# Third patterns of the integer exponential made in place by an adding DMA, with a newly searched order of work, in a fused attention and gated-FFN kernel

## The chip, the cores and the metric

The kernel runs on one core of a Trainium2 chip. The metric is the device time of one execution in microseconds (us). The engines are PE (matmul), ACT (activations, here nearly all exponentials), DVE (vector), POOL (GpSimd) and SP (which here only issues DMAs); each works through its own list of instructions in order, and semaphores order the engines among each other.

## The reference

`x` is 2048 x 512 in bf16. The result mixes an attention block and a gated feed-forward block by a gate for each row:

```python
g = sigmoid((x * gate_w).sum(-1, keepdims=True))
# attention: 32 heads of 16
qkv = x @ wqkv                       # 2048 x 1536
scores = einsum("bhqd,bhkd->bhqk", q, k) * 16 ** -0.5
o = einsum("bhqk,bhkd->bhqd", softmax(scores), v)
a = o @ wo
# feed-forward, F = 1376, without a nonlinearity
b = ((x @ w_gate) * (x @ w_up)) @ w_down
return g * a + (1 - g) * b
```

The exponentials of the scores are the bulk: 32 heads x 2048 x 2048.

## The kernel before

**Tiles.** PE is used as eight tiles of 64 rows by 32 columns. An operation of the helper `pe64` (L1616, its matmuls are recorded at L1620) is four matmuls, one for each column group, in row half 0 or 1; the two halves run beside each other. All products have 512 columns and land in one of eight PSUM banks. Bank 7 holds the attention output of the group in work, the others serve scores and the remaining products.

**Groups and steps.** The attention is 32 groups: four chunks of 512 queries, four blocks of eight heads, and two halves of such a block (four heads). A group has 16 steps, one for each tile of 128 keys, 512 steps in all. A step makes four score tiles of 128x512 (one for each head, `scores`, L1625) and from them four tiles of exponentials, which PE then multiplies with the values (`pv`, L1646).

**Two ways to an exponential.**

- Kind A: ACT reads one or two PSUM banks and writes exp as bf16 (`exp`, L1718). The four tiles are multiplied with the values once (`ps<-PT,Vp`, `ps<-xT,Vp` and so on: the results lie wherever room is, in `PT` and in the bytes of weights and inputs that are no longer needed). That is 8 matmuls a step.
- Kind D: DVE adds a constant to the scaled score and stores it as int16 (`dpass`, L1754); these 16 bits read as bf16 are a rough exponential, "pattern 0". Patterns 1, 2 and 3 are pattern 0 plus 32, 64 and 96 in int16, each in a buffer of its own, made by DVE (`copy`, L1760, one instruction of 128x2048 or half of it) or by POOL (L1764, two int16 taken as one int32). PE multiplies pattern 0 with the values (`Vp`) and patterns 1 to 3 with values scaled by 2^(-v/4) (`Vs`), so that the four rough curves average out. That is 32 matmuls a step, 24 of them on `Vs`. Only the key tiles in `dks` (six of 16) may take this way. The buffers are the eight of `DB` and later the bytes of `wv` and `wk`.

**The rest.** The projections, the feed-forward products and the output products are cut into short slices and put between the steps ("fill"). Their PSUM banks are emptied by DVE. For each pair of groups the denominators go through DRAM: two small DMAs, a reciprocal, a write to `rscr`, a broadcast back into `rb` (`rbc`, L1912) and a multiplication on POOL (L1923).

**What sets the order.** The order of each engine's instructions is worked out when the program is built, by a model of the chip in the class `_Sched`. It goes forward in time and at each moment gives each free engine one piece of work. `s_a` and `s_d` place scores for the two kinds of steps, `try_act` an exponential, `dve_pass` a pass, `copy_dve` and `try_pool` the copies, `v_job` a product with the values. Its choices depend on fixed durations and latencies and on the numbers of `PAR`. Most of these are tables of pairs (count, value): the time is cut into entries of 4 us, and each value holds for so many entries. Some that matter here: `dl` (how many steps of a group may be of kind D), `dend` (how near to the end of a group no new D step begins), `alook`, `dlook` (how many scores may be ahead of their readers), `acc` (below). The products of a group with the values wait until the group's turn in bank 7. The program then has exactly this order on each engine, with a semaphore wait for each dependence; on the chip an engine never passes over an instruction that is not ready.

**The adding DMA.** The code for it is in the kernel before, but with `acc` at 0 it is never used. Where the number of D steps of a group is at or below `acc`, the step's pattern 3 gets no buffer of its own. Its copy leaves the list (`next_d`, L218), and when pattern 0 has been read by both copies and by both its products (five references, `y_unref`, L506), POOL issues a DMA that adds a constant row of 96 to the buffer in place (`acc_pool`, L960, `accum`, L1768):

```python
def acc_pool(self):
    e, deps, _ = self.accq.pop(0)
    op = self.hw.accum(e.buf, deps + [self.last4]) if self.hw else None
    self.pool_v = self.lock_v = self.now + self.par["aiss"]                  # 0.9
    t = self.dma_v = max(self.pool_v + self.par["alat"], self.dma_v + 2.65)  # 3.9
    for r in (0, 1):
        self.vq[r].append((t, e, 3, [op]))      # the products with pattern 3, from t on

def accum(self, buf, deps):
    src = bass.AP(c.tensor, c.offset, [[0, 128], [1, 2048]])
    return self.P.dma("pool", lambda e: e.dma_start(self.db[buf], src, accum_op=ALU.add), ...)
```

`last4` is DVE's last copy before it in the planned order; POOL waits for it. With `acc` set, the prologue also writes the constant row to DRAM (a memset on POOL, two small DMAs on SP), and `rbc` waits for that.

Of the kernel before, what the change touches and what calls it, by code (L numbers as in the profile page):

```python
# [136 lines left out]
class _Sched:  # L137
# [167 lines left out]
    def s_a(self, r):  # L305
# [20 lines left out]
        t = self.now + 0.385 + 0.056  # L326
# [6 lines left out]
    def s_d(self, r):  # L333
# [22 lines left out]
        t = self.now + 0.385 + 0.056  # L356
# [363 lines left out]
    def try_act(self):  # L720
# [51 lines left out]
        dur = 0.833e-3 * 512 * n + 0.051  # L772
# [10 lines left out]
        t = self.now + dur + 0.12 + 0.05  # L783
# [75 lines left out]
    def dve_pass(self, now):  # L859
# [9 lines left out]
        if self.dready and self.dready[0][0] <= now and (mate or not hold):  # L869
# [12 lines left out]
            dur = 0.065 + 0.533 * n  # L882
# [4 lines left out]
            t = self.now + dur + 0.083  # L887
# [661 lines left out]
class _Hw:  # L1549
# [376 lines left out]
    def prologue(self):  # L1926
# [119 lines left out]
        if self.par["acc"]:  # L2046
# [10 lines left out]
 'acc': 0,  # L2057
# [3 lines left out]
 'alook': ((13, 2), (5, 6), (8, 4), (6, 2), (9, 4), (3, 5), (21, 2), (3, 3), (3, 2), (1, 4), (5, 2), (18, 5),  # L2061
# [4 lines left out]
 'amax': ((7, 5), (35, 4), (6, 5), (81, 4), (6, 5), (45, 4)),  # L2066
 'amin': ((7, 3), (6, 2), (13, 4), (6, 2), (9, 3), (3, 2), (6, 4), (2, 2), (22, 3), (28, 4), (5, 3), (18, 4),
          (7, 3), (5, 4), (5, 2), (19, 4), (5, 3), (5, 4), (9, 3)),
 'apick': ((38, 0), (6, 1), (3, 0), (6, 1), (2, 0), (2, 1), (4, 0), (12, 1), (1, 0), (12, 1), (5, 0), (1, 1),
           (5, 0), (14, 1), (11, 0), (25, 1), (14, 0), (6, 1), (13, 0)),  # L2070
 'ares': ((5, 1), (6, 2), (3, 1), (21, 2), (3, 1), (6, 2), (7, 1), (1, 2), (8, 1), (17, 2), (15, 1), (6, 0),
          (24, 2), (9, 1), (9, 0), (22, 2), (18, 1)),
 'await': ((2, 0.05), (10, 0), (6, 0.05), (5, 0), (6, 0.2), (3, 0), (3, 0.2), (3, 0.1), (3, 0.2), (3, 0),
           (7, 0.05), (1, 0.2), (8, 0.05), (11, 0), (3, 0.2), (6, 0), (3, 0.4), (6, 0.05), (3, 0.1), (10, 0),
           (5, 0.4), (4, 0.2), (10, 0.05), (1, 0.4), (3, 0), (15, 0.05), (2, 0.2), (19, 0.05), (3, 0.4),
# [56 lines left out]
 'hold': 1,  # L2132
 'klead': 0.9,
 'kp': [1, 4, 7],
 'lg': [3, 4],
 'mmarg': 0.6,
 'ndum': 7,
 'npre': 0,
# [85 lines left out]
```

## Time and profile before

| | us |
|---|---|
| median of 3 runs | 710.07 |
| lowest, highest | 707.67, 713.38 |
| the profiled execution | 708.04 |
| its span, first to last instruction | 706.3 |
| ACT busy in it | 684.8 |
| DVE busy | 645.9 |
| POOL busy | 450.7 |

The TensorE clock was granted in full (1.00) throughout. A line such as `L1718 ACT ACTIVATE PT<-ps 128x1024 bf16<-128x1024 f32 x328 | 326.8, 1087 | ...` is a group of 328 instructions of line 1718 that read PSUM and write the tile PT; they kept ACT busy for 326.8 us together, and one of them lasted 1087 ns. Instructions of ACT overlap at their ends, so the first number is less than 328 times the second. Since helpers record the operations, the line alone tells little; the names of the tiles tell which step it is.

### The profile page before, as it was taken

To read this page: it belongs to the slowest core of one execution; us is meant where nothing else is said; L and a number is where in the kernel's file an instruction comes from. 1 tells how busy PE (TensorE), PEld (TensorE's weight loads), DVE (VectorE), ACT (ScalarE), POOL (GpSimd) and SP (SyncE) were. 2 spreads that over 40 slices of the span, in tenths; PEclk is the share of its full clock that TensorE was granted. 3 is DMA by queue.
4 is the path that set the end of the run, shared out by engine and by line. 5 is a ranking of instruction groups with operands and counts; after the bars stand their busy time and mean duration, and the time that the engine had idled before them with its cause. 6 is when DMAs were issued, how large, how long until landed. Compare 5 with 4: busy or idle time off the path is not lost.

```text
span 706.3 us, 47734 instructions
## 1 busy us (share of the span) xinstructions
PE 692.3 (98%) x22103; PEld 358.7 (51%) x22103; DVE 645.9 (91%) x1060; ACT 684.8 (97%) x820; POOL 450.7 (64%) x351
## 2 busy tenths in 40 slices
PE   8999999999999999999999999999999999999997
PEld 4564555554444545554554445555553555555553
DVE  5999999899999999999998998999999978989985
ACT  6899999999999999999999999999999999999994
POOL 3365658877464666655675747777666788487630
PEclk9999999999999999999999999999999999999999
DMA  9202341003010100001000010100001010000101
GB/s 156 69 6 57 78 107 36 6 20 94 16 35 5 35 18 23 28 11 28 13 23 23 15 33 19 36 13 13 27 7 40 12 36 24 14 23 18 29 19 33
DMA packets 33752, 22.97 MB, mean 33 GB/s; under 512 B 19500, under 2 KB 30156, under 8 KB 33552
## 3 DMA queue, kind: packets, MB, share of 16 engines
q1 hardware_dynamic: 32416, 18.86, 11.1%
q8 instruction: 173, 2.83, 1.6%
q0 software_dynamic: 176, 0.53, 0.3%
q10 hardware_dynamic: 960, 0.52, 0.3%
q14 instruction: 27, 0.22, 0.1%
HBM read 11.71 MB, written 2.36 MB: 20 GB/s over the span
## 4 chain that ended last, share of the span: by engine, by line
PE 90%; DVE 3%; ACT 3%; issue 1%; DMA 1%; ACTq 0%; DVEq 0%
PE ps L1620 90%; DVE DB L1754 2%; ACT xT L1718 1%; ACT PT L1718 1%; DVE DB L1760 1%; DMA DB<-in_A_x_dram 1%; ACT wu L1718 0%; DVE wv L1754 0%; DVE oc L1830 0%; DVE hT L1902 0%; PE ps L2017 0%; ACTq L1933 0%; DVE wu L1813 0%; ACT wd L1718 0%; ACT QM L2030 0%
## 5 line engine op out<-in xcount | busy, mean ns | idle before, releaser
L1620 PE MATMUL ps<-QM,KT 64*32 64x512 bf16 x8192 | 496.6, 379 | 4.2 <-issue 1.3
L1764 POOL TENSOR_TENSOR DB<-DB,cadd 128x512 int32<-128x512 int32 (+1 forms) x207 | 280.2, 1373 | 146.9 <-DVE DB L1760 62.0
L1718 ACT ACTIVATE PT<-ps 128x1024 bf16<-128x1024 f32 (+1 forms) x394 | 358.5, 1016 | 1.6 <-PE ps L1620 0.7
L1754 DVE TENSOR_SCALAR DB<-ps 128x512 int16<-128x512 f32 (+1 forms) x493 | 327.7, 692 | 31.8 <-PE ps L1620 28.3
L1620 PE MATMUL ps<-DB,Vs 64*17 64x512 bf16 x2856 | 261.6, 377 | 0.7
L1718 ACT ACTIVATE xT<-ps 128x1024 bf16<-128x1024 f32 (+1 forms) x270 | 258.6, 1043 | 1.9 <-PE ps L1620 1.7
L1620 PEld LDWEIGHTS ps<-QM,KT 64*32 64x32 bf16 x8192 | 152.2, 89 | 177.9 <-ACT PT L1718 46.9
L1620 PE MATMUL ps<-PT,Vp 64*17 64x512 bf16 x1444 | 204.5, 376 | 0.3 <-issue 0.2
L1620 PE MATMUL ps<-xT,Vp 64*17 64x512 bf16 x1030 | 165.3, 376 | 0.2
L1620 PE MATMUL ps<-xT,wu 64*32 64x512 bf16 x1376 | 111.9, 377 | 0.0
L1620 PE MATMUL ps<-xT,wg 64*32 64x512 bf16 x1376 | 110.5, 377 | 1.0 <-issue 0.9
L1760 DVE TENSOR_SCALAR DB<-DB 128x2048 int16<-128x2048 int16 (+1 forms) x160 | 107.3, 701 | 0.6 <-PE ps L1620 0.2
L1620 PE MATMUL ps<-wd,hT 64*32 64x512 bf16 x1408 | 100.2, 377 | 0.1
L1620 PE MATMUL ps<-DB,Vp 64*17 64x512 bf16 x1000 | 97.0, 377 | 0.6 <-DVE oc L1830 0.2
L1620 PEld LDWEIGHTS ps<-DB,Vs 64*17 64x17 bf16 x2856 | 70.6, 87 | 37.0 <-PE ps L1620 10.5
L1718 ACT ACTIVATE wd<-ps 128x1024 bf16<-128x1024 f32 (+1 forms) x69 | 65.7, 1059 | 0.6 <-PE ps L1620 0.4
L1764 POOL TENSOR_TENSOR DB<-wv,cadd 128x512 int32<-128x512 int32 (+1 forms) x38 | 49.7, 1331 | 24.2 <-DVE wv L1754 9.6
L1620 PEld LDWEIGHTS ps<-PT,Vp 64*17 64x17 bf16 x1444 | 51.2, 87 | 17.9 <-PE ps L1620 4.6
L1764 POOL TENSOR_TENSOR wv<-DB,cadd 128x512 int32<-128x512 int32 (+1 forms) x31 | 42.1, 1371 | 19.7 <-DVE DB L1760 7.8
L1754 DVE TENSOR_SCALAR wv<-ps 128x512 int16<-128x512 f32 x72 | 47.6, 683 | 2.5 <-PE ps L1620 2.1
L1764 POOL TENSOR_TENSOR wk<-DB,cadd 128x512 int32<-128x512 int32 (+1 forms) x30 | 39.4, 1324 | 15.8 <-DVE DB L1760 11.2
L1620 PEld LDWEIGHTS ps<-xT,Vp 64*17 64x17 bf16 x1030 | 40.8, 87 | 11.6 <-PE ps L1620 2.6
(108 smaller groups left out, 839.5 us busy)
## 6 DMA issues: line engine op xcount, KB each, us to landing
rb<-rscr SPq DMA_DIRECT2D x16, 256.0 KB
QM<-qraw SPq DMA_DIRECT2D x124, 16.0 KB, 2.3
oc<-oraw SPq DMA_DIRECT2D x60, 32.0 KB, 2.2
out_dram<-ost SPq DMA_DIRECT2D x12, 128.0 KB, 1.7
wd<-in_B_w_down_dram SPq DMA_DIRECT2D x10, 128.0 KB, 2.5
wu<-in_B_w_up_dram SPq DMA_DIRECT2D x12, 96.0 KB, 2.2
wg<-in_B_w_gate_dram SPq DMA_DIRECT2D x12, 96.0 KB, 2.6
wv<-in_A_wqkv_dram POOLq DMA_DIRECT2D x1, 512.0 KB, 5.2
```

Of the source, the lines that this page charges most:

```text
L1620: o = pe.matmul(dst, lhs, rhs, start=st, stop=sp, tile_position=(64 * r, 32 * cc), skip_group_check=True)
L1718: return self.P.op("act", lambda a: a.activation(dst, src, ACT.Exp, scale=self.ES), deps)
L1754: return self.dve(lambda v: v.tensor_scalar(dst, src, self.YB, 0.0, ALU.add, ALU.max), deps)
L1760: return self.dve(lambda e: e.tensor_scalar(o, a, 32.0 * v, None, ALU.add), deps)
L1764: lambda e: e.tensor_tensor(o.bitcast(I32), a.bitcast(I32), self.cadd[:, v, :].bitcast(I32).to_broadcast([128, n]), ALU.add),
```

## The change

Four constants of the model move by 4 ns from a latency to a duration or the other way, with their sums unchanged. Two new numbers, `mga` (0.04 us) and `mgd` (0.03 us), are added to the moment at which the model takes a score as ready for ACT or for DVE. `acc` becomes a table: 3 in most entries, 0 to 4 in others. All tables of `PAR` are replaced by newly searched ones. No other code is changed.

```diff
 # s_a
-        t = self.now + 0.385 + 0.056
+        t = self.now + 0.385 + 0.056 + self.par["mga"]
 # s_d
-        t = self.now + 0.385 + 0.056
+        t = self.now + 0.385 + 0.056 + self.par["mgd"]
 # try_act
-        dur = 0.833e-3 * 512 * n + 0.051
+        dur = 0.833e-3 * 512 * n + 0.055
...
-        t = self.now + dur + 0.12 + 0.05
+        t = self.now + dur + 0.116 + 0.05
 # dve_pass
-            dur = 0.065 + 0.533 * n
+            dur = 0.069 + 0.533 * n
...
-            t = self.now + dur + 0.083
+            t = self.now + dur + 0.079
 # PAR
- 'acc': 0,
+ 'acc': ((2, 2), (3, 3), (2, 2), (3, 3), (2, 2), (12, 3), (2, 2), (8, 4), (24, 3), (4, 1), (16, 3), (4, 0),
+         (88, 3), (1, 1), (9, 3)),
...
- 'dl': ((2, 3), (3, 4), (2, 6), (5, 4), (5, 6), (3, 5), (62, 6), (5, 4), (7, 6), (5, 5), (3, 6), (5, 4),
-        (10, 6), (5, 5), (5, 6), (4, 5), (5, 6), (1, 5), (10, 6), (5, 4), (9, 6), (10, 5), (9, 6)),
+ 'dl': ((5, 3), (2, 6), (3, 5), (17, 6), (3, 5), (4, 6), (4, 5), (1, 3), (2, 4), (5, 5), (1, 4), (3, 5),
+        (16, 6), (4, 5), (1, 4), (3, 5), (4, 6), (4, 4), (4, 6), (1, 5), (11, 6), (4, 5), (8, 6), (4, 5),
+        (12, 6), (14, 5), (4, 6), (9, 5), (11, 6), (3, 4), (1, 1), (8, 0), (1, 1), (1, 0), (1, 1), (1, 2)),
...
+ 'mga': 0.04,
+ 'mgd': 0.03,
...
```

More of the change, by code (lines that the diff above doesn't have):

```diff
@@ L2071 @@
[L2071 to L2075, printed above, removed]
-           (8, 0), (8, 0.2)),
@@ new lines @@
+ 'amin': ((2, 3), (12, 2), (4, 4), (5, 2), (2, 3), (1, 4), (34, 2), (1, 4), (1, 3), (8, 2), (4, 4), (3, 2),
+          (13, 4), (2, 2), (14, 3), (19, 4), (2, 2), (7, 3), (4, 2), (3, 4), (18, 3), (9, 4), (11, 3),
+          (1, 2)),
+ 'apick': ((7, 0), (17, 1), (2, 0), (6, 1), (17, 0), (3, 1), (17, 0), (1, 1), (4, 0), (8, 1), (20, 0),
+           (16, 1), (9, 0), (7, 1), (4, 0), (26, 1), (16, 0)),
+ 'ares': ((2, 1), (3, 2), (5, 1), (2, 2), (12, 1), (2, 0), (12, 2), (12, 0), (4, 2), (8, 1), (8, 0), (4, 2),
+          (6, 1), (10, 2), (2, 0), (10, 2), (16, 1), (1, 0), (8, 2), (3, 1), (4, 2), (4, 0), (12, 1), (4, 2),
+          (17, 0), (9, 1)),
@@ L2140 @@
  'ov': [[], [], [], []],
- 'pfirst': ((22, 0), (4, 1), (12, 0), (33, 1), (3, 0), (28, 1), (5, 0), (12, 1), (2, 0), (9, 1), (32, 0),
-            (10, 1), (8, 0)),
+ 'pfirst': ((17, 0), (5, 1), (16, 0), (10, 1), (2, 0), (8, 1), (24, 0), (8, 1), (3, 0), (9, 1), (16, 0),
+            (16, 1), (9, 0), (3, 1), (34, 0)),
  'ph': 1,
```

107 lines of the change are left out of this document (53 added, 54 removed), and 24 rows, old and new, of the table PAR.

## The prediction

> **What bounds the kernel now.** The page comes first: its busy shares (part 1) and the chain that ended last (part 4).
>
> ```profile
> span 706.3 us, 47734 instructions
> ...
> PE 692.3 (98%) x22103; PEld 358.7 (51%) x22103; DVE 645.9 (91%) x1060; ACT 684.8 (97%) x820; POOL 450.7 (64%) x351
> ...
> PE 90%; DVE 3%; ACT 3%; issue 1%; DMA 1%; ACTq 0%; DVEq 0%
> ```
>
> Read alone, these lines say that PE is the bound. But a busy PE is a union of overlapping matmuls and says little of how full it is. So the next view is the list of waits, which says who is late for whom.
>
> ```profile
> PEld ps L1620 <- ACT PT L1718: 47.4, 187, 0.8
> PEld ps L1620 <- ACT xT L1718: 35.3, 131, 0.8
> PEld ps L1620 <- DVE DB L1754: 31.7, 130, 0.6
> ...
> ACT xT L1718 <- PE ps L1620: 1.7, 5, 0.5
> ...
> ACT PT L1718 <- PE ps L1620: 0.7, 2, 0.4
> ```
>
> PE's weight loads wait 82.7 us for exponentials of ACT to give a PSUM bank back and 31.7 us for DVE's passes; ACT waits for PE 2.4 us in these two rows. The late one is ACT. Its timeline in the middle of the run shows how close its instructions follow one another:
>
> ```profile
> 354.33 2.91 ACT L1718 ACTIVATE PT<-ps 128x1024 bf16<-128x1024 f32 x3
> 357.10 1.05 ACT L1718 ACTIVATE xT<-ps 128x1024 bf16<-128x1024 f32 x1
> 358.01 1.06 ACT L1718 ACTIVATE PT<-ps 128x1024 bf16<-128x1024 f32 x1
> 358.91 1.07 ACT L1718 ACTIVATE xT<-ps 128x1024 bf16<-128x1024 f32 x1
> 359.82 4.75 ACT L1718 ACTIVATE PT<-ps 128x1024 bf16<-128x1024 f32 x5
> 364.37 3.87 ACT L1718 ACTIVATE xT<-ps 128x1024 bf16<-128x1024 f32 x4
> 367.98 2.08 ACT L1718 ACTIVATE PT<-ps 128x1024 bf16<-128x1024 f32 x2
> 369.92 2.90 ACT L1718 ACTIVATE xT<-ps 128x1024 bf16<-128x1024 f32 x3
> ```
>
> From 354.33 to 369.92 us 17 exponentials start, one every 15.59 / 17 = **0.917 us**, and the closest starts are 0.90 apart (358.01, 358.91). The stretches tell the same of the whole run:
>
> ```profile
> core 0: us, PE busy (x) PEld busy (x) DVE busy (x) ACT busy (x) POOL busy (x), PEclk, DMA share, GB/s
> 0.00:20.00 20.00, 17.52 (x351) 9.49 (x359) 12.73 (x27) 12.94 (x20) 6.53 (x15) 1.00 0.93 146
> 20.00:670.00 650.00, 643.60 (x20768) 333.66 (x20760) 608.94 (x993) 644.85 (x770) 435.44 (x329) 1.00 0.11 29
> 670.00:706.30 36.30, 31.16 (x1008) 15.57 (x992) 24.26 (x41) 27.05 (x32) 8.72 (x8) 0.99 0.08 26
> ```
>
> ACT is busy 644.85 of 650 us between 20 and 670, DVE 608.94. So the time follows the number of steps that ACT has to do, and that number follows from how many steps the other path (DVE, POOL, PE) can take. A new order gains mainly by moving steps off ACT; what it gains in waits alone is small.
>
> **The change part by part.** There are 512 steps (32 groups of 16 key tiles). A step of kind A costs ACT two 128x1024 exponentials; a step of kind D costs DVE four passes, DVE or POOL three copies, and PE 24 matmuls more (three scaled patterns of 8). The count of D comes from those 24:
>
> ```profile
> L1620 PE MATMUL ps<-DB,Vs 64*17 64x512 bf16 x2856 | 261.6, 377 | 0.7
> ...
> L1620 PE MATMUL ps<-wk,Vs 64*17 64x512 bf16 x384 | 37.9, 376 | 0.1
> ...
> L1620 PE MATMUL ps<-wv,Vs 64*17 64x512 bf16 x312 | 30.6, 376 | 0.0
> ```
>
> (2856 + 384 + 312) / 24 = **148 D steps**, 364 A steps, 444 copies. A step moved from A to D frees ACT of 2 x 0.917 = 1.83 us.
>
> *Copies removed.* The new table lets the first D steps of a group make their third pattern in place. It says 3 in most entries, on average 2.9 over the first 170 (of 4 us each); a group has 148 / 32 = 4.6 D steps, so about 2.8 x 32 = 90 of them use the adding DMA. What a copy and a pass cost:
>
> ```profile
> L1754 DVE TENSOR_SCALAR DB<-ps 128x512 int16<-128x512 f32 x486 | 319.5, 685 | 30.3 <-PE ps L1620 26.8
> ...
> L1764 POOL TENSOR_TENSOR DB<-DB,cadd 128x1024 int32<-128x1024 int32 x81 | 152.3, 1893 | 79.2 <-DVE DB L1760 32.7 <-PE ps L1620 27.3 <-DVE DB L1754 13.7
> ...
> L1760 DVE TENSOR_SCALAR DB<-DB 128x2048 int16<-128x2048 int16 x150 | 103.0, 717 | 0.6 <-PE ps L1620 0.2
> ```
>
> Off DVE a copy saves 103.0 / 150 = 0.69 us, off POOL 1.88 us; a pass is 319.5 / 486 = 0.66 us. Ninety copies are therefore worth between 90 x 0.69 = 62 us of DVE and 90 x 1.88 = 169 us of POOL.
>
> *Adding DMAs.* The profile has no adding DMA. The nearest rows are the two transfers that POOL issues now, one of the same 512 KB and one of 1 KB:
>
> ```profile
> L1933 POOL DMA_DIRECT2D gw<-in_gate_w_dram x1 | 0.9, 913 | 0.0
> ...
> L1933 POOL DMA_DIRECT2D wv<-in_A_wqkv_dram x1 | 0.8, 757 | 2.1 <-DMA wk<-in_A_wqkv_dram 2.1
> ```
>
> ```profile
> q0 software_dynamic: 176, 0.53, 0.3%
> ...
> wv<-in_A_wqkv_dram POOLq DMA_DIRECT2D x1, 512.0 KB, 5.2
> ...
> gw<-in_gate_w_dram POOLq DMA_DIRECT2D x1, 1.0 KB, 4.2
> ```
>
> POOL is held 0.76 to 0.91 us by an issue, so 90 cost it 68 to 82 us; I take 75. It gains 169 - 75 = 94 us at most, and at least loses 75 if all the copies that go were DVE's. The transfers are hidden: 0.53 MB took 0.3% of 706 us, about 2.1 us of all 16 engines, 90 of them 190 us or 27% of the span, beside the 0.11 of the stretches; an addition that reads its target too would cost at most twice that and still fit. The latency is bounded by 4.2 us (the 1 KB row) and 5.2 us (the 512 KB row, in the loading phase, where the DMA share is 0.93). The planner puts the product of this pattern 0.9 + 3.9 = 4.8 us behind the start of the issue, inside both ends. I take it as met. The issue waits on POOL for the step's unscaled products and its two copies, so that the copies of later D steps and the normalising multiplications (L1923) queue behind it; who waits for those are PE's scaled products. POOL, at 64%, can stand that as long as the products come in the planned order; I cost it at nothing, and every us that it holds POOL beyond that is copies that go back to DVE at 0.69 for 1.88.
>
> [...]
>
> *D steps gained.* The first pattern that POOL no longer makes pays for copies that DVE makes now: 94 us of POOL are 50 copies, 50 x 0.69 = 34 us of DVE. Another D step costs DVE four passes and about one of the two copies left to it, 4 x 0.66 + 0.69 = 3.3 us. Ends: 0 steps (nothing is converted) and 62 / 3.3 = 19 (all on DVE). I take **6**, a little over half of 34 / 3.3 = 10, because POOL waits for DVE's copies as it is (69.7 us in the row quoted under the rivals), so not all its free time can be filled. PE gets 6 x 24 = 144 matmuls more:
>
> ```profile
> 550.00:600.00 50.00, 49.64 (x1708) 26.08 (x1692) 42.19 (x64) 49.40 (x58) 39.75 (x22) 1.00 0.09 25
> ```
>
> At 1708 per 50 us, the best rate of the stretches that I asked for, all 22103 would need 647 us, so PE has some 59 us of room and hides the 4 us; without that room they would add 4. The new table of D limits is zero for its entries from 672 to 704 us, so the last steps go to ACT; losing one group's 4.6 D steps would cost 4.6 x 1.83 = 8 us, and my 6 is meant after that.
>
> *Reserves of 0.04 and 0.03 us.* No instruction comes or goes; the planner only assumes scores 40 or 30 ns later, and so picks another order. Both ends come from the number of ACT's pairs.
>
> ```profile
> L1718 ACT ACTIVATE PT<-ps 128x1024 bf16<-128x1024 f32 x328 | 326.8, 1087 | 0.9 <-PE ps L1620 0.2
> ...
> L1718 ACT ACTIVATE xT<-ps 128x1024 bf16<-128x1024 f32 x245 | 244.0, 1082 | 1.9 <-PE ps L1620 1.7
> ...
> L1718 ACT ACTIVATE wd<-ps 128x1024 bf16<-128x1024 f32 x66 | 63.9, 1079 | 0.6 <-PE ps L1620 0.4
> ```
>
> Best case, ACT's starts close up from 0.917 to 0.90: (328 + 245 + 66) x 0.017 = 11 us less. Worst case, each pair really starts 0.04 later: 26 us more. ACT's waits for PE above are so small that I take 0. The shifts of 4 ns between duration and latency leave their sums as they are: 0.
>
> *The constant row.* One memset and two small DMAs early, on POOL and SP; the first reader is an adding DMA after the first D steps, and the reciprocal's broadcast on SP (which now also waits for it, with masks and stores queued behind) comes later still. Hidden; if not, it is two small transfers once, below twice the 4.2 us of the 1 KB row.
>
> **Sum.** ACT loses 6 x 1.83 = 11 us. The profiled execution took 708.0 us (span 706.3 and 1.7 around it), so 697 by it. The median of the runs shown, 710.07, lies 2.0 above that execution: **699 us**. The three runs lie between 707.67 and 713.38, so 1% is about the least that a measurement of this kernel tells from no change.
>
> **The rivals.**
>
> ```profile
> POOL DB L1764 <- DVE DB L1760: 69.7, 36, 7.0
> ```
>
> *Late patterns (slower).* PE works in one fixed order. Behind the product of an adding pattern stand scores, and behind those ACT. If the transfer lands after its planned 4.8 us, PE stops there and all follow. No reserve covers this product: the two new ones are for scores. At 5.2 us (the 512 KB row) each is 0.4 us late, 90 x 0.4 = 36 us; less the 11 gained that is +25, 735 us; half absorbed by the scores that ACT has in hand, +7, 717 us. If POOL also finds a DVE copy running (0.69 us each), a chance of one in five (the x150 row alone fills 103 of 706 us, 15%, and smaller rows come on top), that is 90 x 0.2 x 0.69 = 12 us more. It decides from 11 / 90 = 0.12 us of mean stall. For it: the 5.2, and the 69.7 us that POOL waits for DVE's copies already. Against it: that row was taken with the DMA engines 93% busy, and later they are at 11%. [...]
>
> *Nothing converted.* The copies go, POOL idles, and the count of D steps stays at 148, since passes (0.66 us x 592 = 391 us) and not copies fill most of DVE's time. ACT then needs what it needs now: 705 to 714 us.
>
> *More converted.* Ten D steps or more, and starts at 0.90: 710 - 18 - 4 = 688 us or less. POOL's 36% idle speaks for it, the DVE at 91% against.
>
> **How the numbers follow.** The forecast (690 to 703) has 0.42, more converted (under 690) 0.08, nothing converted (703 to 717) 0.20, late patterns (over 717) 0.30. So faster by over 1% 0.50, within 1% 0.20, slower 0.30. The likeliest time is 699. For eight in ten I leave out the best 7% and the worst 13%: 689 to 728, which reaches about as far as the half-absorbed late case with its waits for copies (717 + 12 = 729) and not to the unabsorbed one.
>
> **What would show it.** Right: matmuls on scaled patterns rise from 3552 towards 3700 (by 24 for each D step), exponentials fall by 12 pairs, POOL shows some 90 issues of 0.76 to 0.91 us, queue 0 carries some 47 MB, landings stand at or under 4.8 us, and ACT still starts a pair every 0.91 us. Wrong by lateness: weight loads wait for a DMA on DB, in rows that now do not exist, and ACT's waits for PE grow past 20 us. Wrong by conversion: the count of exponentials stays at 364 steps' worth. The prediction also falls if copies on DVE slow down beside POOL's issues, which would show as a mean above 0.72 us in their row.

## The result, and the profile after

| | before | after |
|---|---|---|
| median, us | 710.29 (4 runs) | 803.52 (4 runs) |
| lowest, highest | 707.67, 713.38 | 796.17, 809.61 |
| ratio after / before, 95% interval | | **1.1276 [1.1183, 1.137]** |

The change makes the kernel 13% slower; the prediction was 699 us, range 689 to 728. The profile of after is of the longest of its four runs, 809.61 us. A run more than 1.5% above the fastest of its kernel is left out of the ratios here and below, so that a ratio can differ a little from the quotient of two medians.

These lines are from the page of after: the span, the busy shares, the granted clock and the share of the DMA engines in 40 slices, two DMA queues (packets, MB, share of the time of 16 engines), the chain that ended last, and the landing of the new transfers.

```profile
span 807.8 us, 47955 instructions
...
PE 720.7 (89%) x22175; PEld 379.8 (47%) x22175; DVE 639.6 (79%) x1044; ACT 690.4 (85%) x825; POOL 441.3 (55%) x388
...
PEclk9999899999999999999999999999999999999999
DMA  8506575536454521445143254442345454145533
...
q0 software_dynamic: 13424, 48.77, 33.1%
...
q8 instruction: 173, 2.83, 1.4%
...
PE 49%; DMA 25%; DVE 9%; issue 7%; POOL 6%; ACT 2%; SPq 1%; ACTq 0%; DVEq 0%; POOLq 0%
...
DB<-cscr POOLq DMA_DIRECT2D x75, 512.0 KB, 6.7
```

Three engines do about as much as before: ACT is busy 690.4 us against 684.8, DVE 639.6 against 645.9, POOL 441.3 against 450.7. PE is busy 720.7 us against 692.3, with only 72 matmuls more; its lower clock, below, may be a part of that. But no engine is full any more. ACT, at 97% the pace of the kernel before, stands at 85%, and the chain, which ran to 90% through PE, now has 25% DMA and 7% "issue" in it. PE stands idle for 807.8 - 720.7 = 87.1 us of the span, against 706.3 - 692.3 = 14.0 before, so 73.1 of the 101.5 us that the span grew are idle time of PE. The list of waits (total us, times, longest) says on whom:

```profile
DVE DB L1754 <- PE ps L1620: 82.6, 103, 3.8
PEld ps L1620 <- issue: 74.4, 103, 4.5
ACT PT L1718 <- PE ps L1620: 58.6, 51, 5.2
POOL OT L1923 <- DMA rb<-rscr: 48.5, 14, 8.3
...
PEld ps L1620 <- DMA DB<-cscr: 33.7, 33, 3.3
PE ps L1620 <- issue: 33.3, 28, 2.5
...
PE ps L1620 <- DMA DB<-cscr: 22.5, 22, 2.8
ACT xT L1718 <- PE ps L1620: 21.5, 29, 2.0
```

The rows of before that answer to three of them were small:

```profile
PEld ps L1620 <- issue: 13.7, 31, 1.6
...
POOL OT L1923 <- DMA rb<-rscr: 4.4, 1, 4.4
...
PE ps L1620 <- issue: 2.8, 7, 1.1
```

The order between the engines has turned round. Before, PE waited for ACT; now ACT (58.6 + 21.5 us) and DVE (82.6) wait for PE. PE itself waits for two things: for the adding transfers, and for "issue", which is the profile's word for time in which the engine waited for nothing that the profile shows. Both stand in two rows, one of the weight loads (PEld) and one of the matmuls (PE), and these two must not be added: one stop can stand in both. In the trace of after 33.2 of PE's 33.3 us of issue lie inside the 74.4 of PEld. The row of PEld is the longer one, because a weight load can be late while earlier matmuls still run (in the stop of the second kernel shown below the weight load is idle for 1.13 us, the matmul for 0.83). So for "issue" it is 74.4 us on the weight loads (13.7 before) and 33.3 on the matmuls (2.8 before); for the transfers 33.7 and 22.5 on `DB`, and 6.6 and 4.3 on `wv`. ACT's timeline in the place that the prediction showed of before has holes of up to 2.58 us, each ended by PE:

```profile
356.13 1.93 ACT L1718 ACTIVATE PT<-ps 128x1024 bf16<-128x1024 f32 x2
360.65 1.02 ACT L1718 ACTIVATE PT<-ps 128x1024 bf16<-128x1024 f32 x1 [2.58 <-PE ps L1620]
362.48 1.02 ACT L1718 ACTIVATE xT<-ps 128x1024 bf16<-128x1024 f32 x1 [0.81 <-PE ps L1620]
```

The groups by shape give the number of D steps:

```profile
L1620 PE MATMUL ps<-DB,Vs 64*17 64x512 bf16 x3008 | 288.7, 389 | 34.0 <-DMA DB<-cscr 22.5 <-issue 9.5 <-POOL DB L1764 1.1
...
L1620 PE MATMUL ps<-wv,Vs 64*17 64x512 bf16 x360 | 37.0, 386 | 5.2 <-DMA wv<-cscr 4.3 <-issue 1.0
...
L1620 PE MATMUL ps<-wk,Vs 64*17 64x512 bf16 x256 | 26.6, 385 | 2.2 <-DMA wk<-cscr 1.1 <-issue 1.0
```

(3008 + 360 + 256) / 24 = 151 D steps, three more than before. The adding DMAs are 75 on `DB`, 10 on `wk` and 7 on `wv`: 92 of the 151 steps.

### The profile page after: what moved, and what is told of

The parts are those of the page before. It is cut to its first block, busy times and chain, and to the rows that moved or that the text cites. A ratio compares the mean times of both kernels' runs of the same rounds, so it can differ in the third digit from the quotient of the medians.

```text
span 807.8 us, 47955 instructions
## 1 busy us (share of the span) xinstructions
PE 720.7 (89%) x22175; PEld 379.8 (47%) x22175; DVE 639.6 (79%) x1044; ACT 690.4 (85%) x825; POOL 441.3 (55%) x388
## 3 DMA queue, kind: packets, MB, share of 16 engines
q0 software_dynamic: 13424, 48.77, 33.1%
q8 instruction: 173, 2.83, 1.4%
## 4 chain that ended last, share of the span: by engine, by line
PE 49%; DMA 25%; DVE 9%; issue 7%; POOL 6%; ACT 2%; SPq 1%; ACTq 0%; DVEq 0%; POOLq 0%
PE ps L1620 49%; DMA DB<-cscr 13%; DVE DB L1754 4%; POOL DB L1764 4%; DMA wv<-cscr 4%; DMA rb<-rscr 2%; DMA wk<-cscr 2%; DMA rscr<-rec 2%; DMA QM<-qraw 2%; DVE DB L1760 1%; DVE wk L1754 1%; SPq L1825 1%; POOL DB L1771 1%; ACT PT L1718 1%; POOL wk L1764 1%
## 5 line engine op out<-in xcount | busy, mean ns | idle before, releaser
L1620 PE MATMUL ps<-QM,KT 64*32 64x512 bf16 x8192 | 519.4, 387 | 16.9 <-issue 8.2
L1718 ACT ACTIVATE PT<-ps 128x1024 bf16<-128x1024 f32 (+1 forms) x392 | 363.0, 1002 | 59.6 <-PE ps L1620 58.6
L1754 DVE TENSOR_SCALAR DB<-ps 128x512 int16<-128x512 f32 (+1 forms) x474 | 315.9, 692 | 85.4 <-PE ps L1620 82.6
L1620 PE MATMUL ps<-DB,Vs 64*17 64x512 bf16 x3008 | 288.7, 389 | 34.0 <-DMA DB<-cscr 22.5
L1764 POOL TENSOR_TENSOR DB<-DB,cadd 128x512 int32<-128x512 int32 (+1 forms) x167 | 225.2, 1401 | 146.8 <-PE ps L1620 73.7
L1718 ACT ACTIVATE xT<-ps 128x1024 bf16<-128x1024 f32 (+1 forms) x267 | 242.0, 972 | 21.9 <-PE ps L1620 21.5
L1620 PE MATMUL ps<-xT,Vp 64*17 64x512 bf16 x964 | 151.6, 383 | 1.8 <-issue 1.7
L1620 PEld LDWEIGHTS ps<-DB,Vs 64*17 64x17 bf16 x3008 | 76.2, 88 | 93.3 <-DMA DB<-cscr 33.7
L1771 POOL DMA_DIRECT2D DB<-cscr x75 | 69.6, 947 | 62.4 <-PE ps L1620 40.3
L1760 DVE TENSOR_SCALAR DB<-DB 128x2048 int16<-128x2048 int16 (+1 forms) x133 | 88.7, 691 | 10.0 <-PE ps L1620 9.5
L1923 POOL TENSOR_TENSOR OT<-oc,rb 128x512 bf16<-128x512 f32 x16 | 20.9, 1308 | 56.4 <-DMA rb<-rscr 48.5
L1754 DVE TENSOR_SCALAR wk<-ps 128x512 int16<-128x512 f32 x64 | 42.4, 686 | 7.8 <-PE ps L1620 7.5
L1620 PEld LDWEIGHTS ps<-xT,wg 64*32 64x32 bf16 x1376 | 36.4, 94 | 22.6 <-issue 9.5
```

The costliest lines, as they stand in the source:

```text
L1620: o = pe.matmul(dst, lhs, rhs, start=st, stop=sp, tile_position=(64 * r, 32 * cc), skip_group_check=True)
L1718: return self.P.op("act", lambda a: a.activation(dst, src, ACT.Exp, scale=self.ES), deps)
L1754: return self.dve(lambda v: v.tensor_scalar(dst, src, self.YB, 0.0, ALU.add, ALU.max), deps)
L1760: return self.dve(lambda e: e.tensor_scalar(o, a, 32.0 * v, None, ALU.add), deps)
L1764: lambda e: e.tensor_tensor(o.bitcast(I32), a.bitcast(I32), self.cadd[:, v, :].bitcast(I32).to_broadcast([128, n]), ALU.add),
L1923: return self.P.op("pool", lambda g: g.tensor_tensor(self.OT[:, bi % 8, :], self.oc[:], self.rb[:], ALU.mult), deps)
```

## The experiments

Two theories stand against each other. **Late patterns:** PE stops where a product waits for its transfer; if nobody waited for it, the time would be that of the order alone. **Load:** the transfers slow PE by their mere presence on the DMA engines, whoever reads them. A third cause, the new order itself, is tested with them. All kernels below keep the order of the changed kernel unless the text says otherwise; ratios are to the kernel before on the same chip, which took 704.3 to 710.0 us.

### The order alone, and the transfers alone

The first kernel issues no transfer, and the products with pattern 3 read the pattern as it is. The second issues the 92 transfers, without the addition, from the constant row to rows of DRAM that nobody reads. In both PE waits for no adding transfer and for none that replaces one.

```diff
 # acc_pool, first kernel
-        op = self.hw.accum(e.buf, deps + [self.last4]) if self.hw else None
+        op = None
-            self.vq[r].append((t, e, 3, [op]))
+            self.vq[r].append((t, e, 3, list(deps)))
 # accum, second kernel (with the same line in vq)
+        dst = self.tscr[128 * self.nt - 128 : 128 * self.nt, :]
-        ... e.dma_start(self.db[buf], src, accum_op=ALU.add) ...
+        ... e.dma_start(dst, src) ...
```

> The changed kernel's order, kept instruction for instruction, but POOL issues no adding transfer; the products with pattern 3 wait for what the transfer would have waited for and read the unshifted pattern (the addition of 96 is left out). Theory 'late' (the transfers land after the moment at which PE's order has their products, median 6.7 us for 4.8 planned): 690 to 710 us, clock back at 1.00. Theory 'traffic' (48 MB of adding transfers slow instruction loading, masks and broadcasts): also 690 to 710. Theory 'order' (the new order is slow by itself, whatever the transfers do): 760 or more.

> The same order; POOL issues 92 transfers of 512 KB at the same places, but plain ones into DRAM rows that nobody reads, and the products with pattern 3 do not wait for them (the addition is left out). 'Late': within 10 us of e1_none, since nobody waits. 'Traffic': 760 to 800, with PE's waits for 'issue' still near 100 us in all. A mixture stands between: what is over e1_none is traffic and POOL's issue, what is under the changed kernel is lateness.

Measured: without transfers 699.33 us, 0.9941 [0.992, 0.9963]; with transfers that nobody waits for 769.59 us, **1.0933 [1.0891, 1.0974]**. The page of the first kernel, and one stretch of it (us, then busy us of PE, PEld, DVE, ACT and POOL, clock, DMA share, GB/s):

```profile
PE 685.1 (98%) x22175; PEld 370.5 (53%) x22175; DVE 629.6 (90%) x1044; ACT 677.4 (97%) x825; POOL 358.7 (51%) x296
```

```profile
20.00:670.00 650.00, 645.72 (x21097) 348.75 (x21088) 601.04 (x989) 644.75 (x782) 345.74 (x275) 1.00 0.11 30
```

In it ACT is busy 644.75 of 650 us, as in the kernel before: without the transfers the new order does what it was made for. The waits of the second kernel and, from its page, queue 0, queue 8 and the chain:

```profile
PEld ps L1622 <- issue: 66.7, 68, 3.5
PE ps L1622 <- issue: 40.7, 37, 3.0
ACT PT L1720 <- PE ps L1622: 35.9, 31, 3.2
...
POOL OT L1927 <- DMA rb<-rscr: 30.0, 9, 6.1
```

```profile
q0 software_dynamic: 13424, 48.77, 22.6%
...
q8 instruction: 173, 2.83, 1.4%
...
PE 74%; issue 7%; DVE 6%; DMA 6%; ACT 3%; POOL 1%; SPq 1%; ACTq 0%; DVEq 0%; POOLq 0%
```

The "issue" waits are about as large as in after (66.7 us on the weight loads and 40.7 on the matmuls, against 74.4 and 33.3), with no product waiting for a transfer; without transfers the same two rows are 3.5 and 0.2. So 70 us (769.59 - 699.33) come with transfers that no instruction reads, and "late patterns" alone can't be the cause. By the pages PE's idle time grows from 697.3 - 685.1 = 12.2 us to 767.6 - 703.8 = 63.8, which is 51.6 of the 70.3 us between the spans; the other 18.7 are a longer busy time of the same 22175 matmuls, at a mean granted clock of 0.984 against 1.00.

What PE waits for there is seen in its timeline. A stop looks like this, in the second kernel:

```profile
150.01 0.39 PE L1622 MATMUL ps<-DB,Vs 64*17 64x512 bf16 x2
151.22 0.39 PE L1622 MATMUL ps<-DB,Vs 64*17 64x512 bf16 x2 [0.83 <-issue]
151.22 0.08 PEld L1622 LDWEIGHTS ps<-DB,Vs 64*17 64x17 bf16 x1 [1.13 <-issue]
```

It is one stop, and it stands in both rows. It falls inside an operation of four matmuls, between its second and its third, where the program has no wait.

Queue 8 is the clue. It carries 173 packets and 2.83 MB in both kernels, 16 KB each, and PE has 22175 matmuls and 22175 weight loads: 44350 / 173 = 256 instructions for each packet. These packets are taken here as PE's own list of instructions, in blocks of 256. In the trace's packets and matmuls of the second kernel, after the first 20 us, PE has 36 stops longer than 0.4 us, 45.6 us together; 31 of them (40.5 us) end 1.1 to 1.7 us after a packet of queue 8 has landed. The packets come a median of 3.9 us apart, so that by chance 0.6 / 3.9, about one in six, would fall there. The packets last about 1.0 us with and without load; but 37 of them come more than 5 us after the one ahead, against 11 in the kernel before. The reading taken here is that PE stops at the end of a block when the next one has been started late.

Two more counts from the trace bear this out. 29 of the 36 stops are put down to "issue". If PE's weight loads and matmuls are numbered in the order of their starts, all 29 fall on positions 140 to 185 of a block of 256 (18% of it); of the 24 such stops in after it is 23, and of 43 in the kernel with additions in DRAM, below, all. And the queue 8 packet that landed last ahead of each of the 29 began while 4 KB packets of the new transfers were moving or less than 1 us behind them; of all 169 packets of queue 8 after the first 20 us 78 did.

### How much traffic

Three sizes: the issue alone, with 4 KB to DRAM that nobody waits for; the adding transfer cut to a quarter, with its products waiting; and the full transfer as a plain copy over the pattern, waited for too.

```diff
 # 4 KB: to tscr, 16 of 2048 columns, and in vq as in the second kernel
+        ... [[0, 128], [1, 16]] ... e.dma_start(dst, src) ...
 # a quarter
+        ... [[0, 128], [1, 512]] ... e.dma_start(self.db[buf][:, 0:512], src, accum_op=ALU.add) ...
 # plain
-        ... e.dma_start(self.db[buf], src, accum_op=ALU.add) ...
+        ... e.dma_start(self.db[buf], src) ...
```

> As e2_traffic (same order, 92 issues by POOL, nobody waits, the addition left out), but each transfer moves 4 KB instead of 512 KB. If what e2_traffic lost against e1_none (70 us) is the bytes on the DMA engines: 697 to 706 us, and PE's waits for 'issue' fall under 25 us. If it is POOL being held by the issue, and the copies behind it late: 740 or more.

> As the changed kernel, products waiting for the adding transfer, but it adds to 512 of the 2048 columns only (128 KB instead of 512; three of four tiles of pattern 3 stay unshifted). 'Traffic' and 'late' together: landings at 4 to 4.8 us, so hardly a product late, and a quarter of the bytes, so a quarter of the 70 us: 705 to 730. If the count of transfers matters and not their size: 770 or more.

> The same order and the same 512 KB transfer from the same DRAM row into the same buffer, waited for as before, but it overwrites instead of adding (pattern 3 is then the constant row). If the addition makes the landing slow: landings fall to 4.2 to 5.2 us and the time to 700 to 730. If it is the size, the queue or POOL's lock: landings stay at 6 us or more and the time at 780 or more.

| transfer | ratio | landing, us | q0 share | issue waits of PEld / PE, us |
|---|---|---|---|---|
| none | 0.9941 [0.992, 0.9963] | | 0.4% | 3.5 / 0.2 |
| 4 KB, not waited for | 1.0068 [1.0042, 1.0094] | 2.9 | 3.2% | 6.7 / 1.3 |
| 128 KB, adding | 1.0229 [1.0198, 1.0259] | 4.0 | 12.6% | 25.1 / 9.5 |
| 512 KB, plain | 1.0562 [1.0523, 1.06] | 4.2 | 19.3% | 43.2 / 20.6 |
| 512 KB, adding (after) | 1.1276 [1.1183, 1.137] | 6.7 | 33.1% | 74.4 / 33.3 |

The waits behind two rows of the table, first the quarter, then the plain copy, and for this one its queue and its landing:

```profile
PEld ps L1620 <- issue: 25.1, 37, 2.3
...
PE ps L1620 <- issue: 9.5, 14, 1.6
```

```profile
PEld ps L1620 <- issue: 43.2, 53, 3.0
...
PE ps L1620 <- issue: 20.6, 23, 1.6
```

```profile
q0 software_dynamic: 13424, 48.77, 19.3%
...
DB<-cscr POOLq DMA_DIRECT2D x75, 512.0 KB, 4.2
```

Time and issue waits grow with the time that the transfers take of the DMA engines. The quarter and the plain copy land in less than the planned 4.8 us on `DB`, and PE's weight loads wait for them hardly at all (0.2 and 2.6 us); they cost 2.9 and 6.2 points over the order alone all the same. Two other things come out. The 4 KB kernel stands 1.3 points, some 9 us, above the kernel without transfers: that is the price of holding POOL (0.56 us for each issue here, 0.95 in after) and of 92 small transfers, which the prediction had at nothing. The plain copy's 743.60 us fell between the ranges that its two theories named. And the addition itself is dear: the same 512 KB take 19.3% of the engines' time as a copy and 33.1% as an addition, and land in 4.2 or 6.7 us.

### Without the lateness

These two keep the whole change, additions and waits included, but put each product with an added pattern some 20 of PE's operations later in PE's list (fewer where its group ends), so that its transfer has as a rule landed. The first puts it wherever that is; the second only directly behind another product of the same row half.

```diff
+    def later(self, n):          # over the finished list of instructions
+        for x in (the products with an added pattern):
+            # move x behind the next n operations of PE, not past a reader of its result;
+            # second kernel: then on to the next product of the same row half
```

> The changed kernel, whole result, but in PE's list each product that reads an adding transfer stands up to 20 operations (80 matmuls, some 2.5 us) later, as far as the group's end allows. 'Late' then loses its stops: PE's waits for the transfers (64 us in the three largest rows) fall under 20 us. What is left is traffic, so about e2_traffic: 765 to 785 us. If lateness were the larger part: 730 or less. If the stops are only where other delays show: 795 or more.

> As e11_later (whole result, products of the adding transfers 20 or more operations later), but each stands right behind another product of the same row half. e11_later raised the number of changes between the two row halves at the shared bank 7 from 230 to 346; here it stays 230. If e11_later lost to those changes and lateness is a real part: 765 to 790 us, a few per cent under the changed kernel, with waits for the transfers under 20 us. If lateness costs nothing of its own because other delays stand behind it: 795 to 815.

Measured: 824.86 us, 1.1679 [1.1642, 1.1716], for the first, and 791.27 us, 1.1221 [1.117, 1.1273], for the second. The waits of the second:

```profile
PEld ps L1668 <- issue: 76.1, 91, 3.6
...
PE ps L1668 <- issue: 40.9, 37, 2.5
...
PEld ps L1668 <- DMA DB<-cscr: 5.0, 8, 1.6
```

The waits of the weight loads for the adding transfers fall from 33.7 us on `DB` to 5.0 and from 6.6 on `wv` to 1.5, and the ratio goes from 1.1276 to 1.1221, with intervals that overlap. The lateness was real, but taking it away is worth at most a little: while PE waits for a transfer, its next block of instructions has time to come, and without that wait the issue rows grow a little, from 74.4 to 76.1 us on the weight loads and from 33.3 to 40.9 on the matmuls. That explanation of the exchange is argued, not shown. The chain that ended last overstates the lateness: it runs to 25% through DMA in after and to 8% here, and the time is almost the same.

The first kernel was a miss and taught something else. PE's list of waits has hardly any for transfers either, but the kernel changes row halves on the shared bank 7 more often, 346 times against 230, and its list of waits has a new large row:

```profile
PEld ps L1663 <- PE ps L1663: 72.6, 197, 0.7
```

In after this row is 29.4 us, 84 times. In this program a change of half makes the second half wait, by a semaphore, for the first's last product. Against the second kernel, with 24.9 us in this row, 116 more changes go with (1.1679 - 1.1221) x 705.3 = 32 us; if that is all theirs, it is about 0.28 us each, an estimate, since the products of the two kernels also stand at different places.

### The load in the order before, and adding that nobody waits for

The third step is the load without anything else of the change, and the heaviest load without lateness: 92 plain transfers of 512 KB to DRAM in the kernel before, one after every third or fourth copy of POOL; and in the changed order 92 adding ones into six regions of DRAM, not waited for by PE.

```diff
 # before.py, copy on POOL
+        self.nc_ += 1
+        if self.nc_ * 92 // 317 > self.nt:
+            self.nt += 1
+            ...
+            self.P.dma("pool", lambda e: e.dma_start(d, src), [self.r["cst"]], "dtr%d" % (self.nt % 8))
 # changed kernel, accum
+        k = self.nt % 6
+        dst = self.tscr[128 * k : 128 * k + 128, :]
+        ...                                              # six plain transfers on SP fill the regions once
+        ... e.dma_start(dst, src, accum_op=ALU.add) ...
```

> The kernel before, its order kept, whole result, with 92 plain transfers of 512 KB into DRAM rows that nobody reads, issued by POOL behind every third or fourth of its copies. If the traffic theory holds for any order: the same 60 to 80 us as e2_traffic over e7_tiny, so 760 to 790 us, with PE's waits for 'issue' at 80 to 110 us (16 in the kernel before). If it is special to the new order: 705 to 730.

> As e2_traffic (nobody waits, result without the addition), but the 92 transfers of 512 KB add, like those of the changed kernel, to six DRAM regions that are filled once before. If an adding transfer loads the DMA engines more than a plain one (33% against 23% of their time), it delays PE's instruction loads more: 780 to 800 us, and lateness itself is then worth only the 5 to 20 us that are missing to the changed kernel. If both load alike: 765 to 775, and lateness is worth some 25 us.

Measured: 752.93 us, **1.0655 [1.0618, 1.0692]**, in the order before, and 848.61 us, **1.194 [1.185, 1.2031]**, with additions in DRAM. The waits of the two, the order before first, and queue 0 of the second:

```profile
PEld ps L1622 <- issue: 51.2, 70, 2.5
...
PE ps L1622 <- issue: 24.0, 34, 2.1
```

```profile
PEld ps L1622 <- issue: 141.7, 161, 5.4
...
PE ps L1622 <- issue: 94.8, 50, 5.0
```

```profile
q0 software_dynamic: 13424, 48.77, 35.6%
```

The load slows the kernel before as well, so it does not need the new order, though that suffers more from it (0.9941 to 1.0933). Why is not shown: the transfers also come at other places, in 94 bursts in the order before and in 56 longer ones in the new order, if packets less than 0.3 us apart count as one burst. Both results missed the ranges named ahead: 752.93 us lies between the two, and 848.61 above both. And adding transfers that PE never waits for cost more than the change itself, if they go to DRAM. In this kernel 49 of PE's 52 stops over 0.4 us, 100.1 of 105.9 us, end 1.1 to 1.7 us after a packet of queue 8.

### Other shapes of the traffic: the pieces, the source row, the half of the engines

Four more kernels vary the shape of the traffic. The first describes its transfers in pieces of 1 KB in place of 4 KB (to DRAM, not waited for). The second is the whole change with 128 different rows as the source in place of one row read 128 times. The last two put the 512 KB into 8 parts, which by the trace's packets keep 8 DMA engines busy at a time, and issue a transfer of 8 parts of 32 bytes behind or ahead of each, so that by turns the large ones might always fall on the same eight.

```diff
 # pieces of 1 KB
+        src = ... [[0, 128], [512, 4], [1, 512]]; dst = four blocks of 512 columns, 1024 apart
 # 128 rows
+        src = self.cst2[:, :]                             # filled once
 # halves: n = 16 then 1 in one kernel, 1 then 16 in the other
+            src = ... [[0, 8], [0, n], [1, 2048 if n == 16 else 16]]
```

> As e2_traffic (nobody waits, the addition left out), the same 48 MB, but each 4 KB row is written as four pieces of 1 KB into a row with gaps. If PE's instruction loads wait for the packet that is being moved, shorter packets let them in sooner: 715 to 745 us, waits for 'issue' under 60 us. If they wait for all bytes that stand in the queues: 760 to 785, waits for 'issue' near 107 us.

> As the changed kernel, whole result, but the constant stands in DRAM 128 times and each partition reads a row of its own instead of all reading the same 4 KB. If the shared row makes the adding transfer slow: landings fall from 6.7 to near the 4.2 of the plain one, and the time to 730 to 750. If it is the adding: landings stay over 6 us and the time within 2% of the changed kernel, 785 to 815.

> The order of the changed kernel; each of the 92 steps issues two transfers to DRAM that nobody waits for: first one of 512 KB cut into 8 parts, then one of 8 parts of 32 bytes. The addition is left out, as in the run with plain traffic. If each transfer is dealt to the next 8 of the 16 DMA engines in turn, all the large ones fall on the same 8. Theory that PE runs dry because its own instruction loads queue on a loaded engine: of this kernel and its twin with the two transfers exchanged, one has the loads on its loaded half and shows issue waits of PE of 100 us or more and 765 to 800 us, and the other, with the same bytes, shows under 30 us of them and 705 to 725 us. Rival, that what is shared is the memory or the total of bytes: both alike, 750 to 775 us. If the dealing does not alternate or the loads go round all engines, both alike too, which would leave it open.

> The same as its twin with the two transfers of a step exchanged: 8 parts of 32 bytes first, then the 512 KB in 8 parts, so that the large ones all fall on the other 8 DMA engines. Theory of the loaded engine: the opposite of the twin, one of the two at 765 to 800 us with 100 us or more of issue waits, the other at 705 to 725 us with under 30. Rival of shared memory or bytes: both alike, 750 to 775 us.

| kernel | us | ratio | issue waits of PEld / PE, us |
|---|---|---|---|
| pieces of 1 KB | 770.81 | 1.0885 [1.0819, 1.0951] | 77.6 / 38.7 |
| 128 source rows, whole change | 791.39 | 1.1199 [1.1091, 1.1306] | 63.0 / 29.9 |
| 8 parts, large first | 782.67 | 1.1049 [1.0981, 1.1118] | 76.7 / 33.8 |
| 8 parts, small first | 784.28 | 1.0952 [1.0893, 1.101] | 83.0 / 50.0 |

The time of the first is that of 4 KB pieces (1.0933). But the question of shorter packets was not put by it: its trace has the same 13424 packets in queue 0 as the kernel with plain traffic, 11904 of them of 4096 bytes in both. Different source rows land a little earlier (5.8 us on `DB`, 6.5 to 6.6 elsewhere) and stay within the interval of after. In the last two kernels the large transfers do keep 8 engines busy at a time by the trace's packets, and both are alike, a little above the 750 to 775 us that were named for that case. A single engine on which all loads of instructions come, with the large transfers kept off it, is not seen in either. But the small transfer landed 5.1 us after its issue when it came behind the large one and 3.1 when it came ahead, so it is not sure that the two kernels used different halves. The question stays open: the loads may go round all engines, or what is shared lies behind the engines.

### POOL adds in place, and three patterns in place of four

The transfer can be replaced by an addition on POOL (two int16 as one int32), which needs no DMA. Or the fourth pattern can be left out in the 92 steps, and the constant of the pass moved by 53.125 so that the three that are left centre on the exponential; the products of the dropped pattern go too.

```diff
 # accum, POOL adds
+        a = self.db[buf].bitcast(I32)
+        ... e.tensor_tensor(a, a, self.cadd[:, 3, :] (as int32, broadcast), ALU.add) ...
 # three patterns: no transfer, no product with v == 3 in these steps, and in dpass
+        yb = self.YB + (53.125 if three else 0.0)
```

> The same order; POOL makes pattern 3 in place by an addition of its own (128x1024 int32, some 1.9 us) instead of issuing the transfer. The whole result is computed. 'Late' and 'traffic': the pattern is there 1.9 us after POOL starts, well before its 4.8, so 690 to 715; POOL is held 1 us longer each time, 92 us more in all, of which its 45% idle takes most. 'Order': 760 or more.

> The changed kernel's order without the transfers and without the products that read them: in those 92 steps the exponential is averaged over three patterns (0, 1, 2) instead of four, with the pass's constant raised by 53.125 so that three weigh as much as four. PE has 92 x 8 = 736 matmuls less. By 'late' and 'traffic' the order is as good as e1_none showed, and the cut matmuls give PE some slack: 690 to 700 us, 0 to 2% under the kernel before. By 'order': as e1_none or slower.

Measured: 745.76 us, 1.0591 [1.0572, 1.061], for POOL, and 700.28 us, 0.993 [0.9907, 0.9952], for three patterns. The pages, POOL's first; the second fence is of three patterns:

```profile
PE 700.2 (94%) x22175; PEld 368.8 (50%) x22175; DVE 687.2 (92%) x1044; ACT 687.1 (92%) x825; POOL 540.0 (73%) x388
```

```profile
PE 682.4 (98%) x21439; PEld 342.7 (49%) x21439; DVE 629.8 (90%) x1044; ACT 677.2 (97%) x825; POOL 358.7 (51%) x296
...
q8 instruction: 167, 2.74, 1.5%
```

With POOL the issue waits stay small (6.3 us on the weight loads), so the cost is of another kind; the time lies above the 690 to 715 us named for both theories. DVE is busy 687.2 us with its 1044 instructions, against 629.6 in the order alone, and all of that is in its copies (185.8 us against 128.3 in line 1760). Their largest group, first in the order alone, then beside POOL's additions:

```profile
L1760 DVE TENSOR_SCALAR DB<-DB 128x2048 int16<-128x2048 int16 x120 | 80.1, 692 | 2.6 <-PE ps L1620 2.2
```

```profile
L1760 DVE TENSOR_SCALAR DB<-DB 128x2048 int16<-128x2048 int16 x120 | 116.3, 991 | 2.9 <-PE ps L1620 2.0 <-POOL DB L1764 0.5
```

PE's weight loads wait 58.9 us for DVE's passes on `DB` there, against 31.5, and 15.4 for POOL's copies. So DVE falls behind first, while POOL at 73% has time left. Most copies last what they did (the median of the `DB` copies is 687 ns), but the longest takes 2380 ns: single ones are held up. 63 of the 205 copies take over 0.8 us, against 3 in the order alone, and of the 48 that meet one of POOL's new additions in time 39 do.

As a control for the count above: this kernel too has 30 stops of PE over 0.4 us, and only 3 of them fall on positions 140 to 185 of a block.

Three patterns take 736 matmuls off PE and gain nothing that can be told from the 0.9941 of the order alone, since ACT (677.2 us, 97%) sets the pace. Of the kernels here that compute the whole result this is the fastest, 0.7% below the kernel before. It also bears out what queue 8 carries: 736 matmuls and 736 weight loads fewer are 1472 / 256 = 5.75 blocks, and the queue shows 6 packets fewer.

## Why the prediction was wrong, point by point

- **ACT sets the pace.** Right for the order (644.75 of 650 us busy without transfers). What it did not see is that PE, which feeds ACT, depends on something that no row of an engine names.
- **The step that failed: "The transfers are hidden", since 27% of the engines' time "beside the 0.11 of the stretches" still fit.** The size was not far off: 33.1% against 27%, and within the doubling that was allowed. The inference was wrong. Free time on the DMA engines was treated as free, with the transfer itself as the only thing that could be late. But the engines have other users that are waited for. The loads of PE's instructions, 1.6% of the engines' time without transfers, came late by the reading above: the issue waits went from 3.5 to 74.4 us on the weight loads and from 0.2 to 33.3 on the matmuls; the broadcasts of the denominators became 48.5 us of waiting on POOL (4.4 before). Transfers that nobody waits for cost 70 us on the order alone, of which some 9 come without their bytes, by the 4 KB kernel.
- **The landing: "I take it as met".** Wrong: 6.7 us against 4.8, outside the bounds of 4.2 and 5.2, which were rows of plain transfers. The plain copy measured 4.2, so the bounds were right for a copy; the addition was the operation that no row showed, and it had been bounded for its load but not for its latency.
- **POOL's issue.** 0.947 us on average, against the 0.76 to 0.91 of the two rows. Its hold, costed at nothing, is up to 9 us by the 4 KB kernel, where an issue took 0.56 us; at 0.947 it was not measured alone.
- **D steps: 6 taken, 3 came.** 3 x 1.83 = 5.5 us; the order alone measured 704.3 - 699.33 = 5.0. The mechanism was right and the term 11 was twice too large. The copies removed (about 90; 92 came), the reserves and the constant row (0 each) leave no difference beyond that: 5.0 against 5.5. No run took these terms apart, so that errors that cancel, which would be luck, are not ruled out.
- **The rivals.** The slower one had the direction and some of the signs in the trace, but its mechanism is not what decides, so that its direction was right by luck for the most part. The weight loads' mean wait for a transfer is (33.7 + 6.6) / 92 = 0.44 us, well past its deciding point of 0.12, and yet taking nearly all of it out left 1.1221. Its largest price, 735 + 12 = 747 us, was short by 57. "Nothing converted" and "more converted" were both wrong by a few steps.
- **"Wrong by lateness" could not be told from load by the signs that were named.** The weight loads' waits on `DB` did come (33.7 us), but they say that there is lateness and not that it decides; ACT's waits for PE past 20 us came also where nobody waits for a transfer (35.9 us on one row of the kernel with plain traffic). The sign that does tell them apart, the issue rows of PE, was in the list of waits of before (13.7 and 2.8 us), and the prediction did not ask what they were. Its last sign, slower copies on DVE, did not come: their largest group has a mean of 704 ns in after, against 717.
- **Where the later landing comes from, and how long an issue holds POOL.** The plain 512 KB landed in 4.2 us in the same order, which is what the 1 KB row took before, so that the 2.5 us by which the adding one lands later (6.7) come with the addition; and the issues of after, in the view of the tile `DB` (min/median/max ns), were seldom long (14 of the 75 over 1.0 us):

```profile
L1771 POOL DMA_DIRECT2D DB<-cscr x75: 823/868/2617, 24.5 to 783.2; - x75
```

The rest of after against the sum: the order alone gives 0.994, holding POOL 1.3 points, plain traffic that nobody waits for 8.65 points more (from 1.0068 to 1.0933, written to DRAM), and additions with their waits bring it to 1.1276. These are not terms that can be added exactly: the plain copy into SBUF cost less (1.0562) than the one to DRAM, with 19.3% of the engines' time against 22.6%.

The granted clock also fell, to a mean of 0.970 in the profile of after (0.975 to 0.987 in its other three runs) and 0.956 in that of the additions in DRAM, against 1.00 without transfers; one stretch of after shows it:

```profile
100.00:200.00 100.00, 88.21 (x2696) 44.73 (x2681) 77.81 (x127) 81.92 (x89) 55.95 (x56) 0.93 0.56 110
```

It has the lowest clock of the stretches and the highest DMA share after the loading phase. No run separated the clock from the stops, so its part is open; with plain traffic it can't be more than the 18.7 us of longer busy time as far as it acts through longer matmuls, beside 51.6 us of idle time. That the stops are waits for instructions rests on their place in the trace, in time and in the blocks of 256, and on the count of packets. Where a load of instructions is held up, at an engine or behind it, is open: no run changed the loads themselves, and the two that tried to keep the traffic away from them came out alike.

## What to carry to other kernels

A DMA path that looks idle is priced by its other users: before moving work there, ask what else the engines carry that somebody waits for, the engines' own instructions above all where an engine runs through 256 of them in 3.8 us, the median distance of queue 8's packets in the kernel before. Read the "issue" waits of the busiest engine in the profile of before; small as they are (3.5 us on the weight loads in the order alone), traffic can make them grow (66.7 with plain transfers that nobody waits for). And test a transfer first in a kernel where nobody waits for it: that one run tells load from lateness, which the list of waits does not.

## What the runs showed of the hardware that was not expected

- An adding transfer of 512 KB into SBUF takes 1.9 times as much of the DMA engines' time as a plain one (33.1% of 807.8 us against 19.3% of 741.7 for the same 92) and lands in 6.7 us against 4.2; into DRAM, 35.6% of 852.1 us against 22.6% of 767.6, and 6.9 us against 4.8.
- Ninety-two transfers of 512 KB spread over the run, read by nobody, slow a kernel that is bound by ACT by 7 to 10% (1.0655 in one order; 1.0933 against 0.9941 in the other; their issue on POOL is a part of it), with stops of PE at one place of its blocks of 256 instructions (29 of 29 stops put down to "issue" within 18% of the block).
- Copies of 128x2048 on DVE last 991 ns on average where POOL makes 92 additions of 128x1024 more, and 692 ns where it does not; most of those that meet such an addition are held up (39 of 48).
- Products of the two row halves that go in turn to one PSUM bank, each half waiting for the other's last product, cost about 0.28 us a change as an estimate (116 more of them, 32 us).
